# Transposing w3 by row halves, two blocks at a time, and moving a few copies beside it

## The chip, the cores and the metric

The kernel runs on one core of a Trainium2 chip. The metric is the device time of one execution in microseconds (us). Matrix work runs on TensorE, copies and elementwise work on VectorE (DVE), ScalarE (ACT) and GpSimd (POOL); SyncE (SP) issues most transfers.

## What is computed

Sparse attention over 8 batches, 8 heads, 576 positions and a head size of 64, followed by a multiplicative feed-forward layer over the 4608 tokens:

```
scores = q @ k^T / 8      # heads 0-3: causal window of 32; heads 4-7: causal, same position mod 32
attn   = softmax(masked scores);  x = concat_heads(attn @ v)        # 4608 x 512
out    = (((x @ w1) * (x @ w2)) @ w3) @ w_out    # w1, w2: 512x1024, w3: 1024x1024, w_out: 1024x512
```

## The kernel before

Since nothing stands between `w3` and `w_out`, the kernel folds them into one matrix `w34` = `w3 @ w_out` (1024x512), once. Row block `jc` of `w3` (128 rows, 8 blocks) is loaded and cast to fp16 (`load_w3`, tiles `w3n`, on GpSimd), transposed on TensorE into PSUM (`fold_tr`), copied to `w3T` half by VectorE and half by ScalarE, and multiplied with `w_out` (`fold_mm`, L708, two parts `h0`, `h1` of four matmuls of 512 columns).

Attention works on pairs of heads: `pairs[4*b + hp]`, pairs 0 and 1 of a batch local, 2 and 3 strided. p4 to p7 in the text are batch 1, p8 to p11 batch 2. For a pair, q and k are transposed (`ah_T`, `ph_T`, L301 and L393), with the last 64 positions apart (`ah_R`, `ph_R`, the "rest rows"), scores are multiplied (`ah_S`, `ph_S`), exponentiated on ScalarE, masked on VectorE (`ptm`, L360), multiplied with v (PV: `ah_PV`, `ph_PV`, L528 and L383), normalised (`norm`), and transposed into `xT` (`ph_T2`, `ph_T2u`). Batches 0 and 1 go the `ah_` way, ahead of the stream; from batch 2 on (`AHEAD = 2`) the `ph_` way.

The feed-forward layer goes by tiles of 512 tokens: `ab_parts` (L656 `aps`, L665 `bps`, product L668 into `abt`), then `o_parts` (L708 `ops`, copy L719 `osb`, store). The first matrix product waits in PSUM until its copy `asb` is made, on ScalarE, or on VectorE for the first block of tile 1. PSUM is three pools: `psF` (three single banks), `psB` (two double banks, used for scores, `pt` and PV of batch 1's strided pairs) and `psM` (one bank, used for `ah_T` of batch 1, `ah_R`, `ph_R` and `ph_T2`).

TensorE's instructions keep the order in which the program writes them; a scheduler places those of VectorE, ScalarE and most of GpSimd, and each engine then works its list in order. Between 36 and 74 us TensorE's order comes from a list `units` (the folds, then the output parts of tile 0) and a table `plan`, which says after which unit a step of batch 1 goes. After it stands a written-out start of tile 1, and from there `host` spreads a `stream` of attention steps with gaps between the units of a tile.

```
if jc == 0:
    units += [lambda h0=h0: run(h0, *over[0:4]), tr, lambda h1=h1: run(h1, *over[4:])]
else:
    units += [h0] + ([tr] if tr else []) + [h1]
```

Of the kernel before, what the change touches and what calls it, by code (L numbers as in the profile page):

```python
# [8 lines left out]
FP32 = mybir.dt.float32  # L9
# [10 lines left out]
def kernel(  # L20
# [11 lines left out]
    nc = tc.nc  # L32
# [50 lines left out]
    def half_rows(u):  # L83
        return slice(64 * u, 64 * u + 64)
# [311 lines left out]

    def ah_T1c(s, i, dst):
        t = (qT, kT)[i]
        eng = "v" if i and (s.b == 0 or not s.local) else "a"
        if s.local:  # L400
            copy(eng, t[:, s.hp, 0:NM].rearrange("x (p c) -> x p c", c=4),
                 dst.rearrange("x (c p) -> x p c", c=4))
        elif i:
            copy(eng, t[:, s.hp, 0:NM], dst)
        else:
            copy(eng, t[:, s.hp].rearrange("x (c w) -> x c w", w=NW)[:, :, 0:P],
                 dst.rearrange("x (c p) -> x c p", c=4))
# [11 lines left out]
            ah_T1c(s, i, pst[i])  # L419

    def ah_R(b):
        ps = psM.tile([P, 1024], FP16, tag="m", name="rps")
        pvs = [ps[:, 256 * i:256 * i + 256].rearrange("x (g a w) -> x g a w", g=2, a=2) for i in range(2)]
        src = x16[(b, "r")]
        for g in range(4):
            pe(nc.tensor.transpose(pvs[g // 2][:, g % 2].rearrange("x a w -> x (a w)"),
                                   src[:, 2 * g:2 * g + 2].rearrange("p h d -> p (h d)"), id16))
        for i, t in enumerate((qT, kT)):
            copy("av"[i], t[:, 0:2, NM:S], pvs[0][:, :, i])
        copy("v", kT[:, 2:4, NM:S], pvs[1][:, :, 1])  # L430
# [140 lines left out]
    def ph_T2u(s, pt):  # L571
        o = xT[s.hp][:, S * s.b:S * s.b + S]
        dst = [psM.tile([P, 1024], FP16, tag="m", name="t2a"), pt.bitcast(FP16)[:, 1, 512:1024]]

        def tr(u, c, o):
            r = half_rows(u)
            pe(nc.tensor.transpose(dst[u][:, o:o + 64], s.xqs[r, c].rearrange("p h d -> p (h d)"), id16[r, r]))  # L577

        if s.local:
            tr(0, 0, 0)  # L580
            tr(1, 0, 0)
            for c in range(LT):
                if c:
                    tr(0, c, 64 * c)
                if c + 1 < LT:
                    tr(1, c, 32 * c + 64)
            ov = o.rearrange("x (c w) -> x c w", w=LQ)
            outs = [ov[:, :, 32:LQ], ov[:, :, 0:32]]
            ins = [dst[0][:, 0:64 * LT].rearrange("x (c w) -> x c w", w=64),
                   dst[1][:, 32:32 + 32 * LT].rearrange("x (c w) -> x c w", w=32)]  # L590
# [12 lines left out]
        def out(u):  # L603
            copy("a" if s.b == AHEAD and s.local else "v", outs[u], ins[u])
            if tails:
                nc.vector.tensor_copy(out=tails[u][0], in_=tails[u][1])

        out(0)
        return lambda: out(1)

# [131 lines left out]
    def halves(parts):  # L742
# [3 lines left out]

        return [lambda i=i: half(i) for i in range(0, len(parts), 2)]

    def fold_tr(jc):
        js = bass.ds(jc * P, P)  # L750
        ps = psF.tile([P, 1024], FP16, tag="f", name="trp")
        for kc in range(KF):
            pe(nc.tensor.transpose(ps[:, kc * P:(kc + 1) * P], w3n[jc][:, bass.ds(kc * P, P)], id16))  # L753
        pv = ps.rearrange("x (c j) -> x c j", j=P)
        nc.vector.tensor_copy(out=w3T[0][:, :, js], in_=pv[:, 0:4, :])
        nc.scalar.copy(out=w3T[1][:, :, js], in_=pv[:, 4:8, :])

    def fold_mm(jc):
        js = bass.ds(jc * P, P)

        def done(ps):
            copy("va"[jc % 2], w34[:, jc, :], ps)

        return acc_parts(lambda kc: w3T[kc // 4][:, kc % 4, js], lambda kc: woh[:, kc, :], done, 2)


    stream = []
# [7 lines left out]
    def gaps(n):  # L775
        stream.extend([GAP] * n)
# [89 lines left out]
    for p, s in enumerate(pairs):  # L866
        b, i = divmod(p, 4)
        if b < AHEAD:
            continue
        more = p + 1 < len(pairs)  # L870
        g = GAPS[i] if b == AHEAD else (6, 6)
        add(ph_TS, s, pairs[p + 1] if more else None, pairs[p - 1] if p > 4 * AHEAD else None)
        gaps(2)
        if i == 0:
            batch_end[b - 1] = len(stream)
        gaps(g[0] - 2)
        add(ph_PV, s)
        gaps(3)
        if i == 3 and more:
            add(ph_R, b + 1)  # L880
        gaps(g[1] - 3 if more else 2)
    add(ph_T2, pairs[-1])
    gaps(1)
    batch_end[B - 1] = len(stream)
# [54 lines left out]
    def run(*fs):  # L939
        for f in fs:  # L940
            f()

    for jc in range(KF):
        h0, h1 = fold_mm(jc)
        tr = (lambda jc=jc: fold_tr(jc + 1)) if jc + 1 < KF else None
        if jc == 0:
            units += [lambda h0=h0: run(h0, *over[0:4]), tr, lambda h1=h1: run(h1, *over[4:])]
        else:
            units += [h0] + ([tr] if tr else []) + [h1]
    units += halves(o_parts(0))  # L950
    p4, p5, p6, p7, p8 = pairs[4:9]
    def late_homes():
# [4 lines left out]
    def scores(s):  # L957
        both(s)
        ah_S0(s, (0, 1))

    plan = ((16, ah_T, p4), (18, lambda: ah_R(1)()), (20, ah_T, p5), (20, ah_S, p4), (22, ah_S, p5),
            (23, ah_T, p6), (23, late_homes), (24, ah_PV, p4, 0), (25, scores, p6), (25, ah_T, p7), (25, ah_PV, p4, 1),
            (26, ah_PV, p5, 0), (27, scores, p7), (27, ah_PV, p5, 1), (27, ph_T2, p4), (28, ph_TS, None, p8),
            (29, ph_T2, p5), (29, ah_PV, p6, 0), (30, ah_PV, p6, 1), (31, ah_PV, p7, 0))
    for i, u in enumerate(units, 1):
        u()
        for x in plan:
            if x[0] == i:
                x[1](*x[2:])
# [2 lines left out]
    load_vX(2)  # L972
    tile1 = ab_parts(1) + o_parts(1)
    tile1[0]()
    ah_PV(p7, 1)
    ph_T2(p6)
    tile1[4]()
    tile1[2]()
    ph_T2(p7)
    stream[pos[0]]()  # L980
    for i in (1, 3, 5, 6, 7):
        tile1[i]()
    pos[0] += 7
    tile1 = tile1[8:]
# [49 lines left out]
```

## Time and profile before

| | |
|---|---|
| three runs | 271.82, 273.5, 275.29 us; median 273.5 |
| the profiled execution | 272.68 us, its span 271.0 us |
| TensorE busy | 259.7 us (96%), granted clock 1.0 |
| VectorE, ScalarE, GpSimd busy | 153.9, 142.2, 98.2 us |
| transfers | 48.68 MB, mean 180 GB/s |

The profile is one execution. A row of the timeline merges neighbouring instructions of a line: start, time from the first start to the last end, engine, line, operation, output and inputs, count; a bracket tells idle time before it and what ended it. On TensorE the end holds a modelled tail, so neighbouring rows overlap and starts are the better measure.

### The profile page before, as it was taken

How to read it: one execution, taken by the hardware profiler on the slowest of the kernel's cores; microseconds unless marked ns; L12 is line 12 of the kernel's file. 1: busy time of each engine (PE TensorE's matmuls, PEld its weight loads, DVE VectorE, ACT ScalarE, POOL GpSimd, SP SyncE). 2: the span in 40 equal slices, each digit the busy share in tenths (PEclk: the TensorE clock that was granted, in tenths of full speed). 3: DMA queues.
4: the chain of work that ended last, by engine and by line, in shares of the span. 5: the costliest groups of instructions: out<-in, count | busy, mean ns of one | idle time of the engine just before them, and what ended most of it. 6: DMA issues, size and time to landing. Idle time of an engine off the chain costs nothing.

```text
span 271.0 us, 6732 instructions
## 1 busy us (share of the span) xinstructions
PE 259.7 (96%) x2655; PEld 138.1 (51%) x2655; DVE 153.9 (57%) x369; ACT 142.2 (52%) x304; POOL 98.2 (36%) x119
## 2 busy tenths in 40 slices
PE   2999999999999989999999999999999999999995
PEld 1664465655655545554555555555555554444442
DVE  6362543354677766767676777777857753321330
ACT  2683434577657556555655665555565644333322
POOL 5586787868147104620561076017400000000000
PEclk9999999999999999999999999999999999999999
DMA  7999999997696229544952694379231013003004
GB/s 222 295 333 383 411 417 329 256 243 230 199 276 204 96 87 288 180 132 143 280 180 89 183 257 155 118 227 270 73 116 41 0 41 116 0 34 124 0 12 147
DMA packets 61100, 48.68 MB, mean 180 GB/s; under 512 B 31804, under 2 KB 52492, under 8 KB 61068
## 3 DMA queue, kind: packets, MB, share of 16 engines
q1 hardware_dynamic: 57036, 40.97, 49.7%
q10 hardware_dynamic: 4032, 7.28, 7.1%
q8 instruction: 21, 0.34, 0.5%
q14 instruction: 11, 0.09, 0.1%
HBM read 38.80 MB, written 9.44 MB: 178 GB/s over the span
## 4 chain that ended last, share of the span: by engine, by line
PE 91%; ACT 3%; DMA 2%; DVE 1%; issue 1%; SPq 0%; ACTq 0%
PE ops L708 27%; PE bps L665 23%; PE aps L656 22%; PE sps L383 3%; PE t2a L577 2%; PE pt L301 2%; PE sps L348 2%; DMA st<-in_k_dram 2%; PE tps L393 2%; PE sps L471 1%; PE sps L483 1%; PE ps L551 1%; PE trp L753 1%; PE xpl L528 1%; ACT xT L562 1%
## 5 line engine op out<-in xcount | busy, mean ns | idle before, releaser
L656 PE MATMUL aps<-xT,w1h 128*128 128x512 f16 (+1 forms) x288 | 73.7, 376 | 0.5 <-ACT xT L562 0.5
L665 PE MATMUL bps<-xT,w2h 128*128 128x512 f16 (+1 forms) x288 | 73.1, 376 | 0.0
L91 POOL CAST t<-st 128x1024 f16<-128x1024 f32 (+1 forms) x46 | 45.3, 994 | 68.5 <-DMA st<-in_q_dram 43.5
L668 DVE TENSOR_TENSOR abt<-bps,asb 128x512 f16<-128x512 f32 (+1 forms) x72 | 48.6, 679 | 36.2 <-PE bps L665 34.7
L88 ACT COPY asb<-aps 128x512 f32<-128x512 f32 (+1 forms) x71 | 41.4, 585 | 51.2 <-PE aps L656 45.5
L708 PE MATMUL ops<-w,abt 128*128 128x512 f16 x280 | 67.1, 379 | 0.0
L665 PEld LDWEIGHTS <-w2h 128*128 128x128 f16 x288 | 27.1, 98 | 31.0 <-issue 0.7
L656 PEld LDWEIGHTS <-w1h 128*128 128x128 f16 x288 | 26.5, 98 | 28.9 <-issue 1.3
L708 PEld LDWEIGHTS <-abt 128*128 128x128 f16 x280 | 25.2, 98 | 26.1
L719 ACT COPY osb<-ops 128x512 f32<-128x512 f32 x35 | 20.9, 599 | 22.6 <-PE ops L708 22.6
L371 ACT ACTIVATE pte<-sps 128x1024 f16<-128x1024 f32 (+1 forms) x24 | 24.4, 1018 | 13.0 <-PE sps L348 12.6
L543 DVE TENSOR_TENSOR xqs<-sps,rcp 128x768 f16<-128x768 f32 (+1 forms) x24 | 21.4, 891 | 0.8
L360 DVE TENSOR_TENSOR ptm<-pte,maskE 128x1152 f16<-128x1152 f16 (+2 forms) x16 | 12.1, 765 | 7.5 <-ACT pte L371 6.7
L708 PE MATMUL ops<-woh,w3T 128*128 128x512 f16 x64 | 15.6, 379 | 0.0
L88 ACT COPY qT<-pt 128x224 f16<-128x224 f16 (+4 forms) x40 | 15.0, 425 | 0.2 <-PE pt L309 0.2
L90 DVE COPY kT<-pt 128x512 f16<-128x512 f16 (+4 forms) x28 | 11.4, 417 | 6.5 <-ACT kT L88 4.7
L360 DVE TENSOR_TENSOR ptm<-pte,maskX 126x1152 f16<-126x1152 f16 x12 | 10.2, 852 | 8.4 <-ACT pte L371 8.4
L232 POOL CAST v16L<-st 96x768 f16<-96x768 f32 x16 | 13.2, 825 | 4.5 <-DMA st<-in_v_dram 1.7
L383 PEld LDWEIGHTS <-ptm 128*128 128x128 f16 (+1 forms) x264 | 11.1, 98 | 6.1 <-DVE ptm L360 1.4
L260 POOL CAST v16X<-st 126x1024 f16<-126x1024 f32 x6 | 6.8, 1133 | 17.5 <-DMA st<-in_v_dram 17.5
L91 POOL COPY v16L<-v16L 32x640 f16<-32x640 f16 x16 | 12.4, 779 | 1.0
L90 DVE COPY xT<-t2a 128x252 f16<-128x252 f16 (+1 forms) x21 | 8.2, 390 | 8.0 <-PE t2a L577 7.8
(123 smaller groups left out, 280.7 us busy)
## 6 DMA issues: line engine op xcount, KB each, us to landing
st<-in_q_dram SPq DMA_DIRECT2D x16, 512.0 KB, 4.8
st<-in_k_dram SPq DMA_DIRECT2D x16, 512.0 KB, 5.7
st<-in_moe_w_dram SPq DMA_DIRECT2D x16, 512.0 KB, 9.9
out_dram<-osb ACTq DMA_DIRECT2D x27, 256.0 KB, 2.0
st<-in_v_dram SPq DMA_DIRECT2D x32, 144.0 KB
st<-in_v_dram SPq DMA_DIRECT2D x24, 112.0 KB, 2.4
st<-in_moe_w_out_dram SPq DMA_DIRECT2D x4, 512.0 KB, 11.8
out_dram<-osb SPq DMA_DIRECT2D x8, 256.0 KB, 5.4
```

Of the source, the lines that this page charges most:

```text
L88: return nc.scalar.copy(out=out, in_=in_)
L90: return nc.vector.tensor_copy(out=out, in_=in_)
L91: return nc.gpsimd.tensor_copy(out=out, in_=in_)
L360: nc.vector.tensor_mul(o.rearrange("p (a x) -> p a x", x=x), i.rearrange("p (a x) -> p a x", x=x), _ap(s.mask, lo, [[s.mask.ap[0][0], s.kr ...
L371: nc.scalar.activation(out=pv[0:kr, :, lo:hi], in_=src, func=AF.Exp, bias=0.0, scale=scale)
L383: pe(nc.tensor.matmul(s.ps[:, h, c * 65:c * 65 + 65], s.ptm[0:s.kr, c0:c0 + P], s.v[0:s.kr, 2 * (s.hp % 2) + h, c, :], start=True, stop=True))
L543: nc.vector.tensor_mul(s.xqs[0:w, c0:c0 + l].rearrange("p i h d -> p h i d"), xv[:, :, :, 0:D], _ap(rcp, 0, [[rcp.ap[0][0], w], [LT, 2], [ ...
L656: pe(nc.tensor.matmul(st["a"][:, 0:nt], w1h[:, ci, bass.ds(jc * P, P)], xT[ci][:, tok], start=(ci == 0), stop=(ci == KM - 1)))
L665: pe(nc.tensor.matmul(st["b"][:, 0:nt], w2h[:, ci, bass.ds(jc * P, P)], xT[ci][:, tok], start=(ci == 0), stop=(ci == KM - 1)))
L668: nc.vector.tensor_mul(abts[tch][:, jc, skip:], st["b"][:, 0:nt], st["asb"][:, 0:nt])
L708: pe(nc.tensor.matmul(st["ps"], lhs(ci), rhs(ci), start=(ci == 0), stop=(ci == KF - 1)))
L719: nc.scalar.copy(out=osb, in_=ps)
```

## The change

- `fold_tr` stays for blocks 0 and 1. Blocks 2 to 7 are transposed two at a time by a new `fold_tr2`: each 64-row half apart, 32 instructions of 64 columns for two blocks, into two tiles of `psB` instead of one of `psF`, the halves of a block in two banks. One engine copies a whole block (VectorE the even one, ScalarE the odd one), 1024 elements. `w3T` is laid out block by block. In the unit list the two transposes stand ahead of both parts of an odd `jc` instead of one between the two parts of each `jc`, so there are 28 units instead of 31.
- `plan` is renumbered for the shorter list; `ah_R` of batch 1 and the transposes of p5 lie one unit after the other; the PV of p7's first half goes out of the table into the written-out part.
- The last unit of tile 0's output stands between `ph_T2(p6)` and `ph_T2(p7)` and no longer ahead of tile 1; the first two `bps` matmuls of tile 1 (`tile1[2]`) stand behind the scores of p8.
- `ah_T1c`: kT of batch 1's local pairs is copied by VectorE instead of ScalarE. `ah_R` of batch 1 uses `psB` instead of `psM`. `ph_T2u`: xT of p9 is copied by VectorE instead of ScalarE.
- `ph_R` of batch 3 stands one gap after `ph_PV` of p11 instead of three.

```diff
     def ah_T1c(s, i, dst):
-        eng = "v" if i and (s.b == 0 or not s.local) else "a"
+        eng = "av"[i]
...
     def ah_R(b):
-        ps = psM.tile([P, 1024], FP16, tag="m", name="rps")
+        if b:
+            ps = psB.tile([P, 2, NB], FP32, tag="big", name="rps").bitcast(FP16)[:, 0]
+        else:
+            ps = psM.tile([P, 1024], FP16, tag="m", name="rps")
...
-            copy("a" if s.b == AHEAD and s.local else "v", outs[u], ins[u])
+            copy("a" if s.b == AHEAD and s.hp == 0 else "v", outs[u], ins[u])
...
+    def fold_to(jc, lo, hi):
+        return w3T[jc // 4].rearrange("p c j -> p (c j)")[:, (jc % 4) * DF + lo:(jc % 4) * DF + hi]
+
+    def fold_tr2(j0):
+        pts = [psB.tile([P, 2, NB], FP32, tag="big", name=f"trp{j}").bitcast(FP16) for j in range(2)]
+        for j in range(2):
+            for kc in range(KF):
+                for u in range(2):
+                    r = half_rows(u)
+                    pe(nc.tensor.transpose(pts[j][:, u, kc * 64:kc * 64 + 64], w3n[j0 + j][r, bass.ds(kc * P, P)],
+                                           id16[r, r]))
+        for j in range(2):
+            copy("va"[j], fold_to(j0 + j, 0, DF).rearrange("x (c u r) -> x u c r", u=2, r=64),
+                 pts[j][:, :, 0:KF * 64].rearrange("x u (c r) -> x u c r", r=64))
...
         add(ph_PV, s)
-        gaps(3)
+        early = 1 if b == AHEAD else 3
+        gaps(early)
         if i == 3 and more:
             add(ph_R, b + 1)
-        gaps(g[1] - 3 if more else 2)
+        gaps(g[1] - early if more else 2)
...
         if jc == 0:
-            units += [lambda h0=h0: run(h0, *over[0:4]), tr, lambda h1=h1: run(h1, *over[4:])]
+            units += [lambda h0=h0: run(h0, *over[0:4]), lambda: fold_tr(1), lambda h1=h1: run(h1, *over[4:])]
+        elif jc % 2 and jc + 1 < KF:
+            units += [lambda j=jc + 1: fold_tr2(j), h0, h1]
         else:
-            units += [h0] + ([tr] if tr else []) + [h1]
+            units += [h0, h1]
...
-    plan = ((16, ah_T, p4), (18, lambda: ah_R(1)()), (20, ah_T, p5), (20, ah_S, p4), (22, ah_S, p5),
-            (23, ah_T, p6), (23, late_homes), (24, ah_PV, p4, 0), (25, scores, p6), (25, ah_T, p7), (25, ah_PV, p4, 1),
-            (26, ah_PV, p5, 0), (27, scores, p7), (27, ah_PV, p5, 1), (27, ph_T2, p4), (28, ph_TS, None, p8),
-            (29, ph_T2, p5), (29, ah_PV, p6, 0), (30, ah_PV, p6, 1), (31, ah_PV, p7, 0))
-    for i, u in enumerate(units, 1):
+    plan = ((15, ah_T, p4), (16, lambda: ah_R(1)()), (17, ah_T, p5), (17, ah_S, p4), (19, ah_S, p5),
+            (20, ah_T, p6), (20, late_homes), (21, ah_PV, p4, 0), (22, scores, p6), (22, ah_T, p7), (22, ah_PV, p4, 1),
+            (23, ah_PV, p5, 0), (24, scores, p7), (24, ah_PV, p5, 1), (24, ph_T2, p4), (25, ph_TS, None, p8),
+            (26, ph_T2, p5), (26, ah_PV, p6, 0), (27, ah_PV, p6, 1))
+    for i, u in enumerate(units[:-1], 1):
...
     tile1[0]()
+    ah_PV(p7, 0)
+    tile1[4]()
     ah_PV(p7, 1)
     ph_T2(p6)
-    tile1[4]()
-    tile1[2]()
+    units[-1]()
     ph_T2(p7)
     stream[pos[0]]()
-    for i in (1, 3, 5, 6, 7):
+    for i in (2, 1, 3, 5, 6, 7):
         tile1[i]()
```

More of the change, by code (lines that the diff above doesn't have):

```diff
@@ L747, in halves @@
         return [lambda i=i: half(i) for i in range(0, len(parts), 2)]
+    def fold_to(jc, lo, hi):
+        return w3T[jc // 4].rearrange("p c j -> p (c j)")[:, (jc % 4) * DF + lo:(jc % 4) * DF + hi]
     def fold_tr(jc):
-        js = bass.ds(jc * P, P)
-        ps = psF.tile([P, 1024], FP16, tag="f", name="trp")
+        ps = psF.tile([P, DF], FP16, tag="f", name="trp")
         for kc in range(KF):
             pe(nc.tensor.transpose(ps[:, kc * P:(kc + 1) * P], w3n[jc][:, bass.ds(kc * P, P)], id16))
-        pv = ps.rearrange("x (c j) -> x c j", j=P)
-        nc.vector.tensor_copy(out=w3T[0][:, :, js], in_=pv[:, 0:4, :])
-        nc.scalar.copy(out=w3T[1][:, :, js], in_=pv[:, 4:8, :])
+        for i in range(2):
+            copy("va"[i], fold_to(jc, i * NT, i * NT + NT), ps[:, i * NT:i * NT + NT])
+    def fold_tr2(j0):
[9 more added lines that the diff above has]
+                 pts[j][:, :, 0:KF * 64].rearrange("x u (c r) -> x u c r", r=64))
     def fold_mm(jc):
-        js = bass.ds(jc * P, P)
         def done(ps):
             copy("va"[jc % 2], w34[:, jc, :], ps)
-        return acc_parts(lambda kc: w3T[kc // 4][:, kc % 4, js], lambda kc: woh[:, kc, :], done, 2)
+        return acc_parts(lambda kc: fold_to(jc, kc * P, kc * P + P), lambda kc: woh[:, kc, :], done, 2)
     stream = []
@@ L944 @@
         h0, h1 = fold_mm(jc)
-        tr = (lambda jc=jc: fold_tr(jc + 1)) if jc + 1 < KF else None
         if jc == 0:
-            units += [lambda h0=h0: run(h0, *over[0:4]), tr, lambda h1=h1: run(h1, *over[4:])]
+            units += [lambda h0=h0: run(h0, *over[0:4]), lambda: fold_tr(1), lambda h1=h1: run(h1, *over[4:])]
+        elif jc % 2 and jc + 1 < KF:
+            units += [lambda j=jc + 1: fold_tr2(j), h0, h1]
         else:
-            units += [h0] + ([tr] if tr else []) + [h1]
+            units += [h0, h1]
     units += halves(o_parts(0))
```

## The prediction

> **What bounds the kernel now.** I read the page first, its span and its busy times, then the table of stretches, then the timelines of TensorE, VectorE, ScalarE and GpSimd through the first 100 us.
>
> ```profile
> span 271.0 us, 6732 instructions
> PE 259.7 (96%) x2655; PEld 138.1 (51%) x2655; DVE 153.9 (57%) x369; ACT 142.2 (52%) x304; POOL 98.2 (36%) x119
> ...
> 88.00:98.00 10.00, 8.86 (x130) 4.88 (x131) 6.77 (x21) 5.42 (x14) 1.05 (x1) 1.00 0.26 93
> 98.00:124.00 26.00, 26.00 (x303) 13.60 (x302) 17.95 (x42) 15.00 (x36) 9.63 (x11) 1.00 0.60 178
> ```
>
> The profiled execution took 272.68 us, its span 271.0, so 1.7 us lie outside the span. TensorE is busy 96% of it. In the stretch rows the columns are length, busy time of PE, PEld, DVE, ACT and POOL with counts, clock and DMA. From 98 us on TensorE is busy 26.00 of 26.00 us at clock 1.00: what arrives earlier at 98 us arrives earlier at the end, and what is saved on another engine there is worth nothing. The diff touches only 40 to 98 us. There TensorE hardly idles by its busy time (8.86 of 10.00 us is the worst stretch), but "busy" counts the modelled tail of each matmul, so I go by starts: a 512-column matmul issues every 0.216 us (eight from 41.27 to 43.00, rows in A), a 448-column one by its length every 0.19, and what a start is late beyond that is a loss.
>
> **The change part by part.** Minus is a gain.
>
> *A, the transposes of w3.* Blocks 2 to 7 were transposed by eight 128x128 instructions each; now two blocks go together by 32 instructions of 64 rows.
>
> ```profile
> 39.96 1.03 PE L708 MATMUL ops<-woh,w3T 128*128 128x512 f16 x4
> ...
> 41.27 1.89 PE L708 MATMUL ops<-woh,w3T 128*128 128x512 f16 x8
> 43.00 0.61 PE L753 MATMUL trp<-idw,t 128*128 128x128 f16 x8
> 43.44 1.89 PE L708 MATMUL ops<-woh,w3T 128*128 128x512 f16 x8
> ...
> 65.05 1.04 PE L708 MATMUL ops<-w,abt 128*128 128x512 f16 x4
> 66.02 0.41 PE L301 MATMUL pt<-idw,t 64*128 64x64 f16 x16
> 66.26 0.28 PE L309 MATMUL pt<-idw,t 64*128 64x64 f16 x8
> 66.47 1.04 PE L708 MATMUL ops<-w,abt 128*128 128x512 f16 x4
> ```
>
> A block costs 43.44 - 43.00 = 0.44 us before, so a pair 0.88. The row-half form already stands in the kernel at L301: 16 of them take 66.26 - 66.02 = 0.24 us, 15 ns each, since the halves alternate. Going over to it and back costs extra: four matmuls from 65.05 end at 65.92, the first half starts 0.10 later; after the eight at L309 (0.12 us) the next full matmul starts 0.09 late. A pair will cost 0.10 + 32 x 0.015 + 0.09 = 0.67 us. Three pairs give 3 x (0.67 - 0.88) = -0.63. Bounds: the halves have stood in the trace at most 24 in a row and read another tile, so from -1.0 (no switching cost noticed) to +3.2 (they do not overlap; see the rivals). I take the row of the same shape. The copies behind them, one of 1024 elements per block on each engine instead of two of 512 that wait for one another on the same bank, have 1.73 us of matmuls (jc = 1) in front of their first reader, against at most twice the longest copy of 512 from PSUM shown below (0.68), 1.4 us: hidden. If VectorE came to it 0.4 us later, the fold would wait for the excess.
>
> *B and C, the first projections of batch 1.* The transposes of the rest rows move from the single-buffered pool psM to psB, and the two kT copies of the local pairs from ScalarE to VectorE.
>
> ```profile
> 52.37 0.61 PE L753 MATMUL trp<-idw,t 128*128 128x128 f16 x8
> 53.12 0.61 PE L393 MATMUL tps<-idw,t 128*128 128x128 f16 x8
> 53.66 0.44 PE L471 MATMUL sps<-qT,kT 64*128 64x96 f16 x14
> 54.04 1.90 PE L708 MATMUL ops<-woh,w3T 128*128 128x512 f16 x8
> ...
> 55.88 0.61 PE L471 MATMUL sps<-qT,kT 64*128 64x96 f16 x14
> 56.41 1.04 PE L708 MATMUL ops<-woh,w3T 128*128 128x512 f16 x4
> ...
> 52.81 0.27 ACT L88 COPY qT<-rps 128x128 f16<-128x128 f16 x1 [0.42 <-DVE kT L90]
> ```
>
> At 52.37 the eight transposes need 0.44 us, but the next start is at 53.12: 0.31 lost, because psM is held until ScalarE has copied the rest rows, 52.81 + 0.27 = 53.08. With psB the bank is another one: B = -0.30; bounds -0.31 and 0. The scores of p4 take 54.04 - 53.66 = 0.38 us, those of p5 0.53: 0.15 lost on banks whose exponentials ran late behind ScalarE's copies, two of which now leave it. Against it, the second half of p4's scores now needs the bank of the rest rows, perhaps 0.05 late. C = -0.10; bounds -0.15 to +0.20. By the last fold TensorE should be 1.03 us ahead.
>
> *D, the hand-over to tile 1.* The last unit of tile 0 now stands between two ph_T2, and two bps matmuls (0.38 us) move behind the scores of p8. The order of VectorE changes with it: in the built program the copy asb of the first aps stands behind ptm and kT, where it stood ahead of them; the second bps takes the bank of the second aps (freed by ScalarE) and the third aps the bank of the first (freed by that late copy).
>
> ```profile
> 73.36 0.55 PE L656 MATMUL aps<-xT,w1h 128*128 128x448 f16 x2
> 74.13 0.54 PE L656 MATMUL aps<-xT,w1h 128*128 128x448 f16 x2
> 74.63 0.92 PE L665 MATMUL bps<-xT,w2h 128*128 128x448 f16 x4
> 75.51 0.92 PE L656 MATMUL aps<-xT,w1h 128*128 128x448 f16 x4
> ...
> 73.95 0.63 DVE L90 COPY asb<-aps 128x448 f32<-128x448 f32 x1 [0.28 <-PE aps L656]
> 74.58 0.76 DVE L360 TENSOR_TENSOR ptm<-pte,maskE 128x1152 f16<-128x1152 f16 x1
> 75.25 0.68 DVE L90 COPY kT<-pt 128x512 f16<-128x512 f16 x1
> ...
> 73.34 1.03 ACT L371 ACTIVATE pte<-sps 128x1024 f16<-128x1024 f32 x1
> 74.88 0.58 ACT L88 COPY asb<-aps 128x448 f32<-128x448 f32 x1
> ```
>
> Call E the end of the scores and transposes of p8; it is 73.36 here. Before, six matmuls of 0.19 end at E + 1.14, the second bps starts at 74.63 = E + 1.27 and the third aps at 75.51 = E + 2.15: 0.25 us lost, both waits for asb. After, eight matmuls end at E + 1.51. ScalarE's asb ends at 74.88 + 0.58 = E + 2.10, so the second bps starts there and four of them end at E + 2.86. VectorE starts ptm at E + 1.22 and kT at E + 1.89; kT holds it 0.60 (74.58 to 75.25 is 0.67 for the longer ptm), asb takes 0.63 more and ends at E + 3.12. The third aps starts at E + 3.15, where pure issue would put it at E + 2.27: 0.88 lost against 0.25, so +0.63. ScalarE also gets the output copy ahead of the xT copy of p7, which delays the exponentials by about 0.1, and the first PV of p7 comes sooner behind kT of p8's rest rows, another 0.1. The stall ahead of the second ph_T2 stays about as it was. D = +0.80; bounds +0.40 (the copies find gaps) and +1.60 (the second bps too waits for VectorE, 0.76 later).
>
> *E, one xT copy pair from ScalarE to VectorE* (pair p9).
>
> ```profile
> 87.19 0.59 PE L708 MATMUL ops<-w,abt 128*128 128x512 f16 x2
> 87.93 0.48 PE L383 MATMUL sps<-v16X,ptm 126*128 126x65 f16 x10
> ...
> 87.12 0.76 DVE L360 TENSOR_TENSOR ptm<-pte,maskX 126x1152 f16<-126x1152 f16 x1 [1.43 <-ACT pte L371]
> ...
> 85.28 0.48 ACT L88 COPY xT<-t2a 128x384 f16<-128x384 f16 x1 [0.51 <-PE t2a L577]
> ```
>
> Two matmuls from 87.19 end at 87.62; PV starts at 87.93, after ptm (87.12 + 0.76 = 87.88). Ahead of the exponentials ScalarE does this xT copy and later a second one between them, some 0.3 us in all, which go to VectorE, whose next job is that ptm. E = -0.30; bounds -0.31 and 0.
>
> *F, the rest rows of batch 3, two units earlier.*
>
> ```profile
> 94.59 0.39 PE L615 MATMUL rps<-idw,t 128*128 128x128 f16 x4
> 94.82 0.59 PE L708 MATMUL ops<-w,abt 128*128 128x512 f16 x2
> 96.55 0.20 PE L577 MATMUL t2a<-idw,xqs 64*128 64x64 f16 x1 [1.14 <-DVE kT L90]
> ...
> 95.36 0.56 ACT L88 COPY qT<-rps 128x128 f16<-128x128 f16 x4 [0.41 <-PE rps L615]
> ...
> 95.95 0.54 DVE L90 COPY kT<-rps 128x128 f16<-128x128 f16 x4 [1.37 <-ACT qT L88]
> ```
>
> Two matmuls from 94.82 end at 95.25; ph_T2u waits for psM until kT is copied, 95.95 + 0.54 = 96.49, and starts at 96.55. With the switch of 0.10 that is 1.20 lost. Now six matmuls (1.30 us) stand behind the transposes instead of two: they go four matmuls sooner, at 93.73, ScalarE follows at about 94.1 (it need no longer do an output copy first), kT ends at about 95.2, and TensorE arrives at 95.35. F = -1.15; bounds -1.20 and -0.90, since the cover is only 0.1 us longer than the chain.
>
> Moved transfers: one output store goes later past loads of batch 3 in SP's queue, and in POOL's queue the copy of abt moves one cast up; the casts they delay by up to 1 us are used over 4 us later. Nothing.
>
> Sum: -0.63 - 0.30 - 0.10 + 0.80 - 0.30 - 1.15 = -1.68. On the profiled execution that is 272.68 - 1.7 = 271.0 us; the median of the three runs, 273.5, stands 0.8 above that execution, so the forecast is 271.8.
>
> **The rivals.**
>
> *1. The halves don't run side by side (slower).* Place: the 96 half transposes. With h the spacing of two of them, A = 96 h + 3 x 0.19 - 2.64, against -1.05 from all else; the kernel gets slower from h = 33 ns. If the weight loads set the pace as for full blocks (0.44 / 8 = 55 ns), A = +3.2, the sum +2.2 and the time 275.7.
>
> ```profile
> L301 PEld LDWEIGHTS <-t x96: 92/95/96, 66.0 to 97.2; 64*128 64x128 f16 x96
> ...
> L665 PEld LDWEIGHTS <-w2h 128*128 128x128 f16 x288 | 27.1, 98 | 31.0 <-issue 0.7
> ```
>
> For it: a load of 64 rows takes 95 ns (median), one of 128 rows 98, so twice as many loads are no cheaper each. The Trainium skill, "TensorE: Matmul & The Clock Gate", section "LDWEIGHTS (loading the stationary operand)", says just this: the time goes by the columns of the weights, not by the rows. The trace agrees in the two rows above. Against it: at L301 those 95 ns loads still let transposes start 15 ns apart. Chance 0.05.
>
> *2. The hand-over costs more.* If both waits of D fall on VectorE and F's thin cover fails, D = +1.6 and F = -0.9: the sum is -0.63, time 272.9. If besides B and C bring nothing, -0.23: 273.3. For it: VectorE's queue is in order, and every job ahead of asb waits for ScalarE. Against: the bank of the second bps is freed by ScalarE. Chance 0.15.
>
> *3. Earlier demand meets late data (no change).* The second block of each pair is needed 3 to 4 us sooner.
>
> ```profile
> 37.75 1.04 POOL L91 CAST t<-st 128x1024 f16<-128x1024 f32 x1 [0.20 <-DMA st<-in_moe_w_dram]
> ```
>
> This is block 3: cast by 38.79, transposed at 43.00 so far, and needed at 39.96, where the first pair now stands. A load later by 3 us would stall TensorE 1.8 us, all of the gain: 273.5. Against: blocks 5 and 7 have more room, and the casts run at an even 1.25 us. Chance 0.07.
>
> **How the numbers follow.** Forecast (sum between -2.6 and -0.9) 0.70; rival 1 0.05, rival 2 0.15, rival 3 0.07; 0.03 for a larger gain. Adding the ends without rival 1 gives -2.6 (A -1.0, B -0.30, C -0.15, D +0.40, E -0.31, F -1.20) and +0.5 (A -0.4, B 0, C +0.2, D +1.6, E 0, F -0.9), so 270.9 to 274.0 about the median. The three runs lie 271.82 to 275.29, so a median of three can be a microsecond off: 269.7 to 274.3. Two per cent, about what a measurement of this kernel can tell from no change, is 5.5 us: no case reaches it. Rival 1 at its full price with an unlucky draw, or a change of the clock that no row hints at, leave 0.03 on either side.
>
> **What would show it.** In the changed profile: transposes trp of 64 columns about 15 ns apart, a pair in 0.67 us; no gap ahead of the second ah_T; the last fold ending about 1.03 us sooner; a wait of about 0.65 us ahead of the second bps of tile 1 and of 0.25 ahead of the third aps; PV of p10 without a gap; no idle time of TensorE by kT of rps; and from 98 us on the same rows, 1.7 us earlier. The forecast is wrong if a pair takes over 1 us, if the second bps waits over 1.5 us, or if new gaps of TensorE appear after 98 us.

## The result and the profile after

The changed kernel takes 271.9 us (median of 20 runs, 271.2 to 275.9) where the kernel before takes 273.5 (20 runs, 271.6 to 275.8): ratio 0.9953, 95% interval 0.9938 to 0.9968. One of the 20 runs of the changed kernel, the 275.9, was a slow one (recorded clock 0.994) and is left out of the ratio. The change is worth 1.6 us, far inside 2%. The profiled execution took 271.57 us against 272.68.

The page of the changed kernel and its table of stretches (length, busy PE, PEld, DVE, ACT, POOL with counts, clock, DMA):

```profile
span 269.9 us, 6821 instructions
...
88.00:98.00 10.00, 10.00 (x128) 5.25 (x127) 7.67 (x22) 6.56 (x16) 1.63 (x3) 1.00 0.34 115
```

The stretch from 88 to 98 us, 8.86 of 10.00 busy before, is now full. From 186 to 196 us TensorE is busy 9.93 of 10.00 us: it was late twice there, which comes back below.

TensorE's timeline of the changed kernel, the rows that answer to those of the prediction (start, length, engine and line, operation; L708 is now L711, L656 L659, L665 L668, L471 L474, L577 L580, L615 L618):

```profile
40.25 0.64 PE L768 MATMUL trp<-idw,t 64*128 64x64 f16 x32
40.82 3.63 PE L711 MATMUL ops<-woh,w3T 128*128 128x512 f16 x16
...
52.36 0.61 PE L393 MATMUL tps<-idw,t 128*128 128x128 f16 x8
52.90 0.45 PE L474 MATMUL sps<-qT,kT 64*128 64x96 f16 x14
53.28 1.90 PE L711 MATMUL ops<-woh,w3T 128*128 128x512 f16 x8
55.11 0.44 PE L474 MATMUL sps<-qT,kT 64*128 64x96 f16 x14
55.49 1.04 PE L711 MATMUL ops<-woh,w3T 128*128 128x512 f16 x4
...
74.44 0.92 PE L668 MATMUL bps<-xT,w2h 128*128 128x448 f16 x4 [0.62 <-ACT asb L88]
75.33 0.92 PE L659 MATMUL aps<-xT,w1h 128*128 128x448 f16 x4
...
87.01 0.59 PE L711 MATMUL ops<-w,abt 128*128 128x512 f16 x2
87.44 0.47 PE L383 MATMUL sps<-v16X,ptm 126*128 126x65 f16 x10
...
93.23 0.39 PE L618 MATMUL rps<-idw,t 128*128 128x128 f16 x4
93.45 1.46 PE L711 MATMUL ops<-w,abt 128*128 128x512 f16 x6
...
96.47 1.03 PE L659 MATMUL aps<-xT,w1h 128*128 128x512 f16 x4
```

A pair of blocks costs 40.82 - 40.25 + 0.10 = 0.67 us. The second ah_T starts at 52.36, where the four matmuls ahead of it (from 51.50, 0.86 us) end: the gap ahead of it is gone. The scores of p4 (52.90) and of p5 (55.11) take 0.38 each. The second bps of tile 1 carries the new wait for ScalarE's asb. Two matmuls from 87.01 are followed by PV of p10 at 87.44 without a gap. Six matmuls from 93.45 cover the rest rows, ph_T2u follows at 94.84, and nothing waits for kT of rps. The first aps of tile 2 is at 96.47, before at 98.17.

Whole runs differ in more than the change, so I cut every trace at two instructions that all kernels have: the first aps of tile 0 and the first aps of tile 2. Up to the first cut all programs are the same; behind the second, too, every engine works the same list of instructions in all of them, but for the casts of e6_split. Each number is a start or a difference of two starts.

| kernel | first aps of tile 0 at | from it to the first aps of tile 2 | from the first aps of tile 2 to the last matmul |
|---|---|---|---|
| before | 19.62 | 78.55 | 169.33 |
| before, second trace (e9_before) | 20.51 | 78.56 | 169.52 |
| changed | 19.82 | 76.65 | 169.66 |
| changed, second trace (t_after) | 19.97 | 76.77 | 170.79 |
| e1_full | 19.50 | 77.58 | 169.83 |
| e2_serial | 19.99 | 77.89 | 169.96 |
| e3_hand, t_hand | 20.03, 19.29 | 76.38, 76.27 | 169.80, 170.17 |
| e4_late_rest | 20.27 | 78.12 | 170.13 |
| t_onlyF | 19.13 | 77.33 | 169.38 |
| e5_psM | 20.36 | 78.13 | 170.47 |
| e6_split | 19.45 | 75.86 | 169.27 |
| e7_xTact | 19.36 | 77.31 | 169.38 |
| e8_kTact | 19.42 | 77.59 | 170.00 |

The middle column is the change: 1.90 and 1.78 us less, where the kernel before repeats itself to 0.01. The first column moves by 1.4 us from run to run in identical code, the last by 1.5 us in code that only e6_split edits. These two are most of the spread of the times.

### The profile page after: what moved, and what is told of

It reads as the page before. It is cut to its first block, busy times and chain, and to the rows that moved or that the text cites. A ratio compares the mean times of both kernels' runs of the same rounds, so it can differ in the third digit from the quotient of the medians.

```text
span 269.9 us, 6821 instructions
## 1 busy us (share of the span) xinstructions
PE 258.7 (96%) x2703; PEld 136.8 (51%) x2703; DVE 155.9 (58%) x370; ACT 140.6 (52%) x297; POOL 99.2 (37%) x119
## 4 chain that ended last, share of the span: by engine, by line
PE 94%; DMA 2%; ACT 1%; SPq 1%; DVE 1%; issue 0%; DVEq 0%
PE ops L711 28%; PE bps L668 23%; PE aps L659 23%; PE sps L383 3%; DMA st<-in_k_dram 2%; PE t2a L580 2%; PE pt L301 2%; PE sps L348 2%; PE tps L393 2%; PE sps L474 1%; PE sps L486 1%; PE ps L554 1%; PE xpl L531 1%; PE ops L739 1%; PE trp L768 1%; SPq L197 1%
## 5 line engine op out<-in xcount | busy, mean ns | idle before, releaser
L659 PE MATMUL aps<-xT,w1h 128*128 128x512 f16 (+1 forms) x288 | 73.7, 376 | 0.5 <-ACT xT L565 0.5
L668 PE MATMUL bps<-xT,w2h 128*128 128x512 f16 (+1 forms) x288 | 73.1, 376 | 0.6 <-ACT asb L88 0.6
L91 POOL CAST t<-st 128x1024 f16<-128x1024 f32 (+1 forms) x46 | 46.1, 1010 | 67.3 <-DMA st<-in_q_dram 53.0
L711 PE MATMUL ops<-w,abt 128*128 128x512 f16 x280 | 67.1, 379 | 0.0
L668 PEld LDWEIGHTS <-w2h 128*128 128x128 f16 x288 | 27.1, 98 | 31.5 <-issue 1.3
L659 PEld LDWEIGHTS <-w1h 128*128 128x128 f16 x288 | 26.6, 98 | 29.2 <-issue 1.3
L711 PEld LDWEIGHTS <-abt 128*128 128x128 f16 x280 | 25.2, 98 | 26.2
L360 DVE TENSOR_TENSOR ptm<-pte,maskX 126x1152 f16<-126x1152 f16 x12 | 11.4, 946 | 7.7 <-ACT pte L371 7.7
L711 PE MATMUL ops<-woh,w3T 128*128 128x512 f16 x64 | 15.3, 380 | 0.0
L90 DVE COPY xT<-t2a 128x384 f16<-128x384 f16 (+1 forms) x22 | 8.5, 388 | 7.9 <-PE t2a L580 7.7
```

The costliest lines, as they stand in the source:

```text
L90: return nc.vector.tensor_copy(out=out, in_=in_)
L91: return nc.gpsimd.tensor_copy(out=out, in_=in_)
L360: nc.vector.tensor_mul(o.rearrange("p (a x) -> p a x", x=x), i.rearrange("p (a x) -> p a x", x=x), _ap(s.mask, lo, [[s.mask.ap[0][0], s.kr ...
L659: pe(nc.tensor.matmul(st["a"][:, 0:nt], w1h[:, ci, bass.ds(jc * P, P)], xT[ci][:, tok], start=(ci == 0), stop=(ci == KM - 1)))
L668: pe(nc.tensor.matmul(st["b"][:, 0:nt], w2h[:, ci, bass.ds(jc * P, P)], xT[ci][:, tok], start=(ci == 0), stop=(ci == KM - 1)))
L711: pe(nc.tensor.matmul(st["ps"], lhs(ci), rhs(ci), start=(ci == 0), stop=(ci == KF - 1)))
```

## The experiments

**A, the transposes by halves.** The first puts whole blocks back into the pairs:

```
-                for u in range(2):
-                    r = half_rows(u)
-                    pe(nc.tensor.transpose(pts[j][:, u, ...], w3n[j0 + j][r, ...], id16[r, r]))
+                pe(nc.tensor.transpose(pts[j][:, 0, kc * P:kc * P + P], w3n[j0 + j][:, ...], id16))
```

> Both blocks of a pair are transposed by eight full 128x128 instructions each, into the same two psB tiles at the same places; copies stay one per block. Theory (the row halves overlap, which is term A): a pair takes 0.88 us from the end of the matmul before it to the next fold matmul, instead of 0.67, so everything behind the third pair starts 0.63 us later than in the changed kernel. Rival (the gain before the last fold came from the earlier place and the larger copies, not from the halves): a pair in 0.67 and nothing later.

The second keeps the halves and does eight upper ones, then eight lower ones:

```
-            for kc in range(KF):
-                for u in range(2):
+            for u in range(2):
+                for kc in range(KF):
```

> The same 32 half transposes, but all eight of the upper half of a block first, then all eight of the lower half. Theory (15 ns apart because upper and lower half alternate): neighbours now use the same rows, a start every 27 to 55 ns, a pair in 1.05 to 1.95 us and everything behind the third pair 1.1 to 3.8 us later. Rival (a half transpose is cheap by itself): 15 ns apart and a pair in 0.67 us as in the changed kernel.

TensorE's timeline, e1_full first, then e2_serial:

```profile
48.52 1.06 PE L766 MATMUL trp<-idw,t 128*128 128x128 f16 x16
49.41 1.03 PE L711 MATMUL ops<-woh,w3T 128*128 128x512 f16 x4
```

```profile
40.42 0.81 PE L768 MATMUL trp<-idw,t 64*128 64x64 f16 x32
41.16 3.63 PE L711 MATMUL ops<-woh,w3T 128*128 128x512 f16 x16
```

Whole blocks: 49.41 - 48.52 = 0.89 us a pair (0.89, 0.90, 0.89 for the three), against 0.67: 0.22 a pair, 0.66 for the three. Halves one after the other: 41.16 - 40.42 + 0.10 = 0.84. This falls between both theories (1.05 or more, or 0.67). With 0.09 for going back to full rows, a half starts (0.57 - 0.09)/32 = 15 ns behind the last on average when they alternate, (0.74 - 0.09)/32 = 20 ns when they don't, and a whole block of 128x128 0.89/16 = 56 ns.

The single starts say why. Alternating, two start 3 ns apart and the next two 29 ns behind the first two. In e2_serial the first five of a pair start about 29 ns apart and the sixth comes 8 ns behind the fifth. The 32 starts fall into four runs of eight with 29 ns between neighbours (39 for the first two): the runs begin at 0, 134, 268 and 403 ns, each when three of the run before it are still to come. That the record at 268 ns is the second block's first transpose is seen by its semaphore wait; it is the fourteenth to start and the seventeenth in the program. So a row half takes one transpose per 29 ns in either order, and the two halves run side by side; written one after the other, they still overlap by three of eight. So the theory's spacing holds on one half (27 ns or more), its price does not. The alternation is what halves the 29 ns. The loads of 64 rows, 95 ns long, don't set the pace in either order.

Behind the folds both kernels lost 0.3 and 0.8 us more near 58 to 61 us, which no transpose explains; its cause is in the part on the mask multiplications.

**D, the hand-over.** In e3_hand and t_hand tile 1 begins with the other of its first two steps, so that the second aps stands between two groups of four bps:

```
-    for i in (2, 1, 3, 5, 6, 7):
+    for i in (1, 2, 3, 5, 6, 7):
```

> In tile 1 the second half of the first aps again comes before the moved bps (list 1, 2, 3, 5, 6, 7). VectorE's list then has asb ahead of ptm and kT, and the second bps waits for that copy. Theory (term D is the place of asb on VectorE): the waits ahead of the second bps (0.62 idle, 0.78 late) and of the third aps (0.13 late) shrink to under 0.15 together, and from PV of p8 on all starts are 0.7 to 0.8 us earlier than in the changed kernel: span about 269.1 to 269.3. Rival (D comes from ScalarE, which does an output copy ahead of xT of p7): the waits stay above 0.5.

VectorE's timeline from 72.5 us on, the changed kernel first, then e3_hand with TensorE's rows:

```profile
73.39 0.76 DVE L360 TENSOR_TENSOR ptm<-pte,maskE 128x1152 f16<-128x1152 f16 x1 [0.91 <-ACT pte L371]
74.06 0.68 DVE L90 COPY kT<-pt 128x512 f16<-128x512 f16 x1
74.67 0.61 DVE L90 COPY asb<-aps 128x448 f32<-128x448 f32 x1
```

```profile
72.35 0.55 PE L659 MATMUL aps<-xT,w1h 128*128 128x448 f16 x2
...
73.87 0.92 PE L668 MATMUL bps<-xT,w2h 128*128 128x448 f16 x4
74.66 0.92 PE L659 MATMUL aps<-xT,w1h 128*128 128x448 f16 x4
...
72.94 0.62 DVE L90 COPY asb<-aps 128x448 f32<-128x448 f32 x1 [0.24 <-PE aps L659]
73.60 0.76 DVE L360 TENSOR_TENSOR ptm<-pte,maskE 128x1152 f16<-128x1152 f16 x1
```

In the changed kernel asb of the first aps is third in VectorE's queue, as predicted, and the third aps starts at 75.33, 3.19 us behind the end of p8's scores (72.14). In e3_hand asb goes first, nothing waits, and the third aps is at 74.66, 2.31 behind (72.35): 0.88 us back. That trace lost 0.57 of it again at the PV of p10 (87.34), behind a mask multiplication of 1.38 us, and t_hand's trace 0.49 at the same place, behind one of 1.30.

**F, the rest rows of batch 3.** e4_late_rest undoes this edit in the changed kernel, t_onlyF makes it alone in the kernel before:

```
-        early = 1 if b == AHEAD else 3
+        early = 3
```

> The rest rows of batch 3 go back to three gaps behind PV of p11 (early = 3). Theory (term F): two matmuls stand behind them again, TensorE is idle about 1.1 us ahead of ph_T2u, by kT of rps, and everything from 97 us on is 1.2 us later than in the changed kernel. Rival (the earlier order only moved the loss elsewhere): the time behind it is less than 0.5 us later.

The two timelines of TensorE, e4_late_rest first:

```profile
95.03 0.59 PE L711 MATMUL ops<-w,abt 128*128 128x512 f16 x2
96.77 0.20 PE L580 MATMUL t2a<-idw,xqs 64*128 64x64 f16 x1 [1.14 <-DVE kT L90]
```

```profile
93.44 1.46 PE L708 MATMUL ops<-w,abt 128*128 128x512 f16 x6
94.83 0.20 PE L577 MATMUL t2a<-idw,xqs 64*128 64x64 f16 x1
```

Undone, two matmuls (0.43 us, and 0.10 for the switch) end at 95.56 and t2a waits until 96.77: 1.21 us. Alone, six matmuls end at 94.74 and t2a follows at 94.83. By the table F alone is worth 78.55 - 77.33 = 1.22, and the rest of the change 0.6 to 0.7.

**The timed comparison.**

> The changed kernel as it is, timed again beside the others of this call. Theory (the terms measured so far: folds -0.65, second rest rows -0.3, kT copies -0.15, hand-over +0.75, xT -0.31, third rest rows -1.2, some loss behind 98 us): 1.1 to 1.9 us under the kernel before, ratio 0.993 to 0.996. Rival, that the gain is taken back in most runs by late mask multiplications behind 98 us: 0 to 0.7 us under, ratio 0.9975 or more.

> Tile 1's first half in the order aps, bps, aps, ph_TS (steps 1, 2, 3) instead of bps first, timed. Theory, that the hand-over's 0.75 us goes and nothing takes its place: 0.6 to 0.9 us under the changed kernel, ratio to the kernel before 0.990 to 0.993. Rival, that a late mask multiplication of p10 (1.38 us in the single look, 0.76 in the changed kernel) takes 0.57 of it back in every run: 0.1 to 0.3 us under the changed kernel, ratio 0.994 to 0.9955.

> The kernel before with one edit alone, the rest rows of batch 3 two gaps sooner. Theory, that this edit is worth its 1.15 to 1.3 us by itself: 1.0 to 1.4 us under the kernel before, ratio 0.995 to 0.9965, and no idle of TensorE by kT of rps ahead of t2a near 96 us. Rival, that the edit pays only together with the others (or that the folds carry the gain): within 0.4 us of the kernel before, ratio 0.9985 to 1.0015.

| kernel | median us | ratio to the kernel before (273.5) | 95% interval |
|---|---|---|---|
| t_after | 272.3 | 0.9951 | 0.9924 to 0.9977 |
| t_hand | 271.0 | 0.9896 | 0.9862 to 0.9931 |
| t_onlyF | 271.5 | 0.9928 | 0.9901 to 0.9954 |

t_hand beats both kernels by its median, 1.3 us under t_after, more than the 0.3 to 0.5 by which the middle column moves, so 271.0 is partly luck; the intervals of the two overlap. t_onlyF can't be told from the whole change. The rivals of t_onlyF and t_hand lie outside the intervals, though the middle of both intervals is a larger gain than the theories gave. For t_hand that leaves a question open: the late PV of p10, its rival's mechanism, stands in both traces of this order (0.57 and 0.49 us), so the traces show half of the 0.88 us or less as kept, and no run shows where the rest of the 1.3 us comes from. t_after keeps to its theory; its one trace lost 1.5 us behind 98 us, so that its rival holds for single runs.

**B, E and C undone one at a time.** Each line is put back as before: the pool of the rest rows of batch 1 (e5_psM), the engine of p9's xT copies (e7_xTact), the engine of the local kT copies (e8_kTact).

```
-        if b:
-            ps = psB.tile([P, 2, NB], FP32, tag="big", name="rps").bitcast(FP16)[:, 0]
-        else:
-            ps = psM.tile([P, 1024], FP16, tag="m", name="rps")
+        ps = psM.tile([P, 1024], FP16, tag="m", name="rps")
...
-            copy("a" if s.b == AHEAD and s.hp == 0 else "v", outs[u], ins[u])
+            copy("a" if s.b == AHEAD and s.local else "v", outs[u], ins[u])
...
-        eng = "av"[i]
+        eng = "v" if i and (s.b == 0 or not s.local) else "a"
```

> The changed kernel with the rest rows of batch 1 back in the ring of one buffer of ah_T. The half unit between ah_T of p4 and the rest rows, and the one between these and ah_T of p5, are all that the copies have. Theory: the rest rows wait 0.6 to 0.7 for kT of p4 (it ends at 51.92 in the changed kernel, TensorE is there at 51.28), ah_T of p5 then 0.2 to 0.7 for the last copy of the rest rows: 0.8 to 1.4 us in two waits. Rival (the price of the prediction): one wait of 0.3 ahead of ah_T of p5 as before.

> The changed kernel with the xT copies of p9 back on ScalarE. Theory: the mask multiplication of p10 starts later, PV of p10 comes 0.2 to 0.35 us late as before (0.31), and nothing else moves. Rival, that ScalarE has room for it in the new order: no wait ahead of PV of p10.

> The changed kernel with the kT copies of the local pairs of batch 1 back on ScalarE. Theory: ScalarE does qT and kT one after the other, the exponentials of p4 run late, and the scores of p5 take 0.53 instead of 0.38 us: 0.1 to 0.2 us. Rival 1, that the shorter distance of the units makes it more: ah_T of p5 or the scores of p4 wait too, 0.4 to 1.0 us. Rival 2, that it was nothing: 0.38 us for both.

TensorE's timeline of e5_psM, e7_xTact and e8_kTact:

```profile
52.52 0.38 PE L426 MATMUL rps<-idw,t 128*128 128x128 f16 x4 [0.54 <-DVE kT L90]
...
53.94 0.61 PE L393 MATMUL tps<-idw,t 128*128 128x128 f16 x8 [0.18 <-ACT qT L88]
```

```profile
86.55 0.59 PE L711 MATMUL ops<-w,abt 128*128 128x512 f16 x2
87.29 0.48 PE L383 MATMUL sps<-v16X,ptm 126*128 126x65 f16 x10
```

```profile
52.51 0.47 PE L474 MATMUL sps<-qT,kT 64*128 64x96 f16 x14
52.91 1.90 PE L711 MATMUL ops<-woh,w3T 128*128 128x512 f16 x8
54.75 0.44 PE L474 MATMUL sps<-qT,kT 64*128 64x96 f16 x14
55.12 1.04 PE L711 MATMUL ops<-woh,w3T 128*128 128x512 f16 x4
```

e5_psM: two waits, of 0.54 us idle ahead of the rest rows and 0.18 ahead of ah_T of p5. By starts, each less that of the first aps of tile 0, the rest rows come 0.70 us later than in the changed kernel and ah_T of p5 1.04. That is inside the theory's 0.8 to 1.4; the rival of one wait of 0.3 falls. In the changed kernel's shorter distances psM would have cost over three times the 0.31 that it cost before. e7_xTact: two matmuls end at 86.98, PV of p10 comes at 87.29: 0.31 late, as before. e8_kTact: the scores of p4 and p5 take 0.40 and 0.37 us although both kT copies are on ScalarE again. Rival 2: the copies are worth nothing at these scores. What else was lost in the middle column (0.94 us in e8_kTact, 0.35 of the 0.66 in e7_xTact, 0.4 of the 1.48 in e5_psM) belongs to the next point.

ScalarE's timeline between the two scores, the kernel before first, then e8_kTact:

```profile
53.48 0.58 ACT L756 COPY w3T<-trp 128x512 f16<-128x512 f16 x1 [0.40 <-DVE w3T L755]
...
54.91 1.23 ACT L511 ACTIVATE pte<-sps 128x640 f16<-128x640 f32 x2
```

```profile
53.58 1.21 ACT L514 ACTIVATE pte<-sps 128x640 f16<-128x640 f32 x2
```

Before, ScalarE copies half of the last block of w3 at 53.48, ahead of qT and kT of p5, and p4's exponentials end at 56.14, 0.26 us behind the start of p5's scores (55.88). In e8_kTact that copy of w3 is done long before, the order of ScalarE is otherwise the same, and the exponentials end at 54.79, 0.04 behind the start of p5's scores (54.75). So the earlier fold is enough to take the wait away. Moving kT alone might have been enough too: without its 0.47 us (54.44 to 54.91) the old exponentials would end at about 55.67, by this estimate ahead of p5's scores. This is read from rows; no run moves either copy alone in the old order.

**What slows the mask multiplications.** Three stretches of three kernels, VectorE and GpSimd together: the changed kernel near 193 us, t_after near 195 us, e8_kTact near 73 us with the aps that follows.

```profile
193.39 1.05 POOL L260 CAST v16X<-st 126x1024 f16<-126x1024 f32 x1 [2.92 <-DMA st<-in_v_dram]
193.40 1.64 DVE L360 TENSOR_TENSOR ptm<-pte,maskX 126x1152 f16<-126x1152 f16 x1 [0.48 <-ACT pte L371]
195.10 0.48 PE L383 MATMUL sps<-v16X,ptm 126*128 126x65 f16 x10
```

```profile
195.00 0.76 DVE L360 TENSOR_TENSOR ptm<-pte,maskX 126x1152 f16<-126x1152 f16 x1 [0.48 <-ACT pte L371]
195.23 1.44 POOL L260 CAST v16X<-st 126x1024 f16<-126x1024 f32 x1 [2.83 <-DMA st<-in_v_dram]
```

```profile
73.03 1.04 POOL L91 CAST t<-st 128x1024 f16<-128x1024 f32 x1 [1.10 <-PE aps L659]
73.45 1.23 DVE L360 TENSOR_TENSOR ptm<-pte,maskE 128x1152 f16<-128x1152 f16 x1 [0.91 <-ACT pte L371]
75.86 0.92 PE L659 MATMUL aps<-xT,w1h 128*128 128x448 f16 x4 [0.44 <-DVE asb L90]
```

The multiplication that starts 0.01 us behind a cast takes 1.64 us, the cast its usual 1.05. Started ahead of the cast, the multiplication takes 0.76 and the cast 1.44. The thirteen traces with casts in one piece hold 312 mask multiplications of 1152 columns from 70 us on. 184 of them started with no GpSimd instruction running and took 0.75 or 0.76 us, all of them. 128 started beside one. Where more than 0.15 us of it were left (107), the multiplication took that rest and 0.60 to 0.61 us, up to 1.64 in all; where less was left (21), 0.76. VectorE's other large jobs don't show it: abt, one of whose inputs is in PSUM, takes 685 to 687 ns on average in all of them. The Trainium skill, "SBUF — State Buffer", section "SBUF: two separate sides", says it in these words: "The shared pair is an exclusive lock, not a bandwidth split"; it counts a VectorE instruction with two SBUF inputs against a GpSimd one that reads SBUF, and whichever starts first keeps it to its end. These rows agree: 1.64 us and 1.05 when the cast starts first, 0.76 and 1.44 when the multiplication does.

The casts wait for loads ("DMA st<-in_q_dram" is their releaser), so where they fall changes from run to run. In e8_kTact such a pair made asb late and the third aps wait 0.44 us, and from 54.60 us on four multiplications took 4.43 us beside a row of casts, with 0.45 us lost right behind them; near 58 us three in e2_serial took 4.11 us, with its extra loss behind them; e7_xTact lost 0.34 at the PV of p11 behind one of 1.25 us, e5_psM 0.42 behind one of 1.29.

e6_split takes the long casts away. It is t_hand, with the casts from batch 3 on in pieces:

```
-                ins = copy(eng, t, st.rearrange("p h c d -> p c h d"))
+                    for c in range(4):
+                        ins = copy(eng, t[:, c], st[:, :, c])
```

(and load_rest by two, load_vL by two and load_vX by four in the same way).

> The order of tile 1 as in t_hand, and GpSimd's casts from batch 3 on cut in two to four instructions each (256 elements instead of 1024). Theory, a lock: a mask multiplication that starts while a GpSimd instruction runs stands until that instruction ends and then takes 0.60 us (up to 1.64 so far, 0.76 alone); with pieces of at most 0.45 us none takes over 1.1 us, and from the first aps of tile 2 to the last matmul it is 169.3 to 169.5 us (169.7 to 170.8 in the eight traces with the changed order, 169.3 and 169.4 in the two with the old one). Rival 1, shared bandwidth: the multiplication is slowed for as long as both run, and pieces change nothing: up to 1.6 us, 169.7 to 170.8. Rival 2, the pieces follow one another so closely that VectorE does not get between them: as rival 1. In time the theory gives 0.3 to 0.8 us under t_hand, ratio to the kernel before 0.987 to 0.990; both rivals 0.990.

Groups by line from 96 us on, the changed kernel, then e6_split (busy us, mean ns, idle time ahead of them), and one of its two longest multiplications:

```profile
L360 DVE TENSOR_TENSOR ptm<-pte,maskX 126x1152 f16<-126x1152 f16 x10 | 9.7, 975 | 6.5 <-ACT pte L371 6.5
L91 POOL CAST t<-st 128x1024 f16<-128x1024 f32 x16 | 17.8, 1119 | 48.9 <-DMA st<-in_q_dram 45.1 <-DMA st<-in_k_dram 3.4
L91 POOL CAST t<-st 128x512 f16<-128x512 f32 x4 | 2.5, 613 | 1.0 <-DMA st<-in_k_dram 1.0
```

```profile
L376 DVE TENSOR_TENSOR ptm<-pte,maskX 126x1152 f16<-126x1152 f16 x10 | 9.1, 910 | 6.4 <-ACT pte L387 6.4
L91 POOL CAST t<-st 128x256 f16<-128x256 f32 x72 | 27.7, 430 | 47.9 <-DMA st<-in_q_dram 34.7 <-PE bps L684 11.7 <-DMA st<-in_k_dram 1.2
...
139.69 1.43 POOL L276 CAST v16X<-st 126x256 f16<-126x256 f32 x4
140.51 1.22 DVE L376 TENSOR_TENSOR ptm<-pte,maskX 126x1152 f16<-126x1152 f16 x1 [0.48 <-ACT pte L387]
```

From the first aps of tile 2 to the last matmul it is 169.27 us, the shortest of all, and no mask multiplication behind it makes TensorE late. The size was missed: the longest still takes 1.26 (1.1 expected); at 140.51 two pieces went through before VectorE did, since the pieces follow one another without a pause. GpSimd pays 27.7 us in 72 pieces where it paid 20.3 in 20 (17.8 for 16 of 1024 columns, 2.5 for 4 of 512), time that it has. Measured 270.0 us (269.4 to 272.7) against 273.2 for the kernel before, ratio 0.9899, interval 0.9856 to 0.9943: under the kernel before by less than 2%, and not to be told from t_hand (0.9896). So the time doesn't decide: the theory gave 0.987 to 0.990 and both rivals 0.990. What speaks for the theory is one trace; in its middle column, too, it needs 0.4 to 0.5 us less (75.86) than the two of the same order with whole casts, and PV of p10 is about 0.1 late instead of 0.49 and 0.57.

**Whether the old order meets casts as well.** The kernel before was traced once more.

> The kernel before once more, for its trace. From the first aps of tile 2 to the last matmul the two traces with the old order so far need 169.33 and 169.38 us, those with the changed order (casts in one piece) 169.38 to 170.79. Theory, that mask multiplications meet casts by chance in either order: this one can lie anywhere in 169.3 to 170.8, and one above 169.6 shows it. Rival, that only the changed order brings them together: 169.3 to 169.4.

It needs 169.52 us: over the 169.4 that the rival gives, under the 169.6 that would have shown the theory. One mask multiplication of 1.27 us at 189.48 cost 0.19. So the old order meets casts too, but in three traces it lost 0.2 us at most, and nine of ten with the changed order (casts in one piece) lost 0.3 to 1.5. For one place the traces show that the change moves a cast towards the multiplication. The last cast of v16X starts 95.1 to 95.8 us behind the first aps of tile 2 in the three traces with the old order, and 96.9 to 98.5 in nine of the ten with the changed one (95.5 in e1_full); the mask multiplication near it starts at 96.8 to 98.3 in all. In four of these nine the cast came first, and the multiplication took 1.45 to 1.64 us. It cost 0.16 to 0.19 us in three of them; for the larger losses near 130 to 140 us the cause of the difference isn't settled.

## Why the prediction was right, and where only by luck

| step | predicted | measured |
|---|---|---|
| A, halves | -0.63 | -0.66: three times 0.22 (e1_full) |
| B, rest rows of batch 1 | -0.30 | -0.31: the gap is gone; 1.04 if it is undone in the new order |
| C, kT copies | -0.10 | -0.15: the scores of p5 are that much shorter, but not by the copies (e8_kTact) |
| D, hand-over | +0.80 | +0.75: TensorE 1.12 ahead at ah_T of p6, 0.37 at PV of p8; 0.88 comes back in e3_hand |
| E, xT of p9 | -0.30 | -0.31 (e7_xTact) |
| F, rest rows of batch 3 | -1.15 | -1.20 to -1.22 (e4_late_rest, t_onlyF) |
| sum | -1.68 | -1.90 and -1.78 (middle column) |

- *Bounds and path.* Right: what came earlier at 98 us was TensorE's to keep, and every step was priced by starts and not by busy time.
- *A.* Size and reason are right: a half takes one transpose per 29 ns, and alternating makes 15 of it. Rival 1 put 55 ns on halves that don't overlap. By e2_serial it would have been 29, so with no overlap at all A would be 96 x 0.029 + 0.57 - 2.64 = +0.71 and the sum -0.34, not +2.2.
- *B, E and F* have their rows and their size. F's cover of 0.1 us, which the prediction worried about, held.
- *C.* The step that failed. The prediction laid 0.15 us at p5 to ScalarE's two kT copies. With the copies back on ScalarE the scores are as short. By the rows of ScalarE term A does it: the copy of w3's last block, 0.58 us, no longer stands ahead of p4's exponentials. The prediction counted the kT copies on top of A where either was enough. By the last fold TensorE was 1.12 us ahead where 1.03 was forecast.
- *D.* Second bps at 2.30 behind the end of p8's scores (2.10 predicted), third aps at 3.19 (3.15). By starts they are 0.79 and 0.13 late. The prediction's own working gives 2.10 - 1.51 = 0.59 and 3.15 - 2.86 = 0.29 (it named 0.65 and 0.25), so the total is right, 0.92 against 0.88, and its split is not: the second bps waits longer for ScalarE's asb, and the third aps less for VectorE's. The +0.75 of the table is the lead of 1.12 us at ah_T of p6 (57.29 and 56.37) less that of 0.37 at PV of p8 (76.26 and 76.09), each start less that of the first aps of tile 0; 0.67 of it is the lateness of 0.92 against 0.25 before, the rest was lost ahead of p8's scores.
- *Rivals 2 and 3.* Neither came: D stayed at half of rival 2's 1.6 and F's cover held; block 3 of w3 was cast by 40.20 in the changed kernel's trace, 0.29 us ahead of its first transpose.
- *Behind 98 us.* The prediction said "the same rows, 1.7 us earlier" and called new gaps there a sign that it was wrong. The changed kernel has two, 0.21 us ahead of an aps at 188.88 and 0.19 ahead of the PV at 195.10, each behind a mask multiplication that met a cast. Its span fell by 1.1 us and not by 1.9: it started 0.2 later, lost 0.33 behind the first aps of tile 2, and ended 0.3 later behind the last matmul. That sign came true, and no row of the prediction allowed for it. The changed order alone doesn't force such gaps, since e7_xTact runs it from there on and needs 169.38 us, as the old order does; but nine other traces of it were 0.3 to 1.5 longer. For the last cast of v16X the traces show a shift towards the multiplication, for the rest it stays open.
- *The number.* 271.8 against 271.9 is closer than the working deserves. The anchor was a median of three runs (273.5, by luck that of twenty), the spread of single runs, 4 us, is over twice the change, and a loss behind 98 us made up for a gain that was 0.1 to 0.2 larger than forecast. The range, too, was drawn loosely: it adds 1.2 us below the sum's ends and 0.3 above, where the microsecond that it names would give 269.9 to 275.0.

## To carry to other kernels

Price a change in TensorE's order by the starts of its instructions and by who is queued ahead of the copy that frees the next bank: all six terms came out within 0.1 us that way, five of them for the reason given. To judge a change smaller than the spread of the runs, cut the traces at instructions that both kernels share and compare the stretch between them; the start and the tail move on their own. Where an instruction of VectorE takes 0.76 us in one run and 1.64 in the next, see what GpSimd was doing when it began.

## What the runs showed of the hardware that was not expected

- Transposes of 64 columns on one row half start 29 ns apart, whole 128x128 ones 56 ns. The two halves run side by side: alternating, a start every 15 ns; eight and eight in turn, every 20, since TensorE begins the second half when three of the first eight are still to start.
- A VectorE multiplication of two fp16 SBUF tensors (1152 columns, 0.76 us) that starts beside a GpSimd instruction with over 0.15 us to go ends 0.60 to 0.61 us behind it, up to 1.64 us in all; begun first, it holds the cast up instead (1.44 instead of 1.05 us).
- The start is not the same from run to run in the same code. In the two traces of the kernel before, one stretch (columns as above) held 35 matmuls and 27, both at a recorded clock of 1.00; what slowed the second is open:

```profile
12.60:14.40 1.80, 1.80 (x35) 1.42 (x34) 0.56 (x2) 1.25 (x3) 1.61 (x4) 1.00 1.16 374
```

```profile
12.60:14.40 1.80, 1.80 (x27) 1.68 (x28) 0.42 (x1) 1.39 (x3) 1.64 (x3) 1.00 1.14 322
```

- GpSimd's cast of 1024 columns takes 1.05 us undisturbed, four of 256 take about 0.36 each (139.69 to 141.12): cutting costs 0.4 us, and two pieces can still pass ahead of a waiting VectorE.
